# An attention and two feed-forward layers on one core: weights unpacked in place and ahead of the first product, with three smaller moves

## The chip, the core and the metric

The kernel runs on one core of one Trainium2 chip. The metric is the device time of one execution in microseconds (us), lower is better. TensorE (PE in the profile) multiplies; VectorE (DVE), ScalarE (ACT) and GpSimd (POOL) do elementwise work; SyncE (SP) mainly starts transfers. Each engine works through its own instructions in order, and waits for the others by semaphores.

## What is computed

```python
x  = attention(q, k, v, mem_k, mem_v)  # 4 batches x 8 heads x 768 positions x 64
#    chunks of 32 queries see 16 + 32 + 8 keys around them and 8 memory keys
x  = x.transpose(0, 2, 1, 3).reshape(3072, 512)
h  = x @ w_in                          # 512 x 2048
g  = maximum(h, 0) + log1p(exp(-abs(h)))
x1 = g @ w_out                         # 2048 x 512
y  = ((x1 @ w_a) * (x1 @ w_b)) @ w_o2  # 512 x 1536, twice, and 1536 x 512
```

The weights arrive as 64-bit floats, so the kernel unpacks them itself.

## The kernel before

The 3072 tokens are worked in 8 tiles of 384. Every product is made from a high and a low part of each operand, by three matrix products (high x high, high x low, low x high).

**Phase 1** (tiles t = 0 to 7, and in each f = 0 to 15): `ph` is one slice of x @ w_in, 12 matmuls (emit_h). The softplus follows on ACT (three activations, L462 to L464) and DVE (L466), ACT and POOL split it into `gh` and `gl` (L445, L446), and two slices later `px` adds it into the four accumulators of x1, 12 matmuls (emit_x1). After slice 15 the accumulators are copied out (`xo`, L484) and sent to DRAM. The next tile's `px` starts in the same four accumulators, so it waits for these copies. In phase 1 PE's order around a change of tiles is ph15, px13, ph0 of the next tile, px14, ph1, px15, ph2, px0. **Phase 2** does the same with w_a, w_b and w_o2, on x1 read back from DRAM.

**Weights.** A weight slice is 512 KB of raw words, in a buffer of the pool `w` (33 buffers, which hold raws, finished weights and much of the first attention). `convert_a` scales the upper words on ACT (L100) and joins upper and lower words on DVE (L102, L103) in a buffer `tmp`, of which there are two; `convert_b` rounds to the high part on ACT (L110) and gets the low part by a subtraction on POOL (L111). Tile 0 needs 32 weights: two are converted before the first `ph`, the others two per slice f. The 36 weights of phase 2 are converted in tile 7 and at the start of phase 2.

**Attention.** Tile 0's is done before the first `ph`, as 6 blocks of 64 queries. Their steps are woven by a table ROUND: round i does step s0 of block i, s1 of block i-1, and so on. s0 turns k and q on PE (`pt`), ACT and DVE copy the turned ones (L281, L285); s1 makes the scores (`scb`) and the exponentials; sn normalizes; s2 turns the result (`pat`); s3 multiplies by v (`pxb`) and places the block in the tile's x. SyncE starts the loads of k and q, ScalarE those of v.

For tiles 1 to 7 it is done as 21 units of 128 queries, three per tile, woven into the products of the tile ahead. A table of times in half slices sets the place of each step: turn (DVE transposes L354 to L357, two copies of the memory keys on GpSimd, L359), scores (`sc` on PE), soft, norm (POOL L334), flip (ten DVE transposes into `af`, L388), values (`pxa` on PE, L402) and place (ACT L409 writes x's high part, DVE L410 the low one). The last unit's place completes the x that the next tile's first `ph` reads.

For tile 0 the program fixes the order on all engines; from tile 1 on it fixes PE's, and a scheduler orders the others.

Of the kernel before, what the change touches and what calls it, by code (L numbers as in the profile page):

```python
# [9 lines left out]
F32 = mybir.dt.float32  # L10
F32R = mybir.dt.float32r
U32 = mybir.dt.uint32
AF = mybir.ActivationFunctionType
ALU = mybir.AluOpType
# [3 lines left out]
TT = 384  # L18
# [1 line left out]
LAG = 2  # L20
STEPS = ((-8, "turn"), (-5.3, "scores"), (-5, "soft"), (-3, "norm"), (-1, "flip"), (-0.9, "flip2"),
         (3, "values"), (3.1, "place"))
START = 2.4
SETS = 1
EARLY_STEPS = ((-6, "turn"), (-4.3, "scores"), (-4.2, "soft"), (-3, "norm"), (-0.7, "flip"), (1.3, "flip2"),
               (2, "values"), (2.9, "place"))
EARLY, EARLY_AT, EARLY_BY = 3, 13, 9
ROUND = ((0, "s0"), (1, "s1"), (2, "sn"), (3, "s3"), (2, "s2"))
CONVERT_AT = {21: "a0", 23: "b0", 25: "a1", 28: "b1"}
W_AT = {3: 1, 5: 2}  # L30
W_BY = (1, 2, 2, 2)
AHEAD = 10
LATE = 4
OUT_TAGS = "eegg"

# [2 lines left out]
def attn_moe_moe2(ctx: ExitStack, tc: tile.TileContext, q, k, v, mem_k, mem_v,  # L38
                  w_in, w_out, w_a, w_b, w_o2, out):
    nc = tc.nc  # L40
    B, H, S, D = q.shape
    M = mem_k.shape[2]
# [3 lines left out]
    P = 128  # L46
    CH, LC, RC = 32, 16, 8
    QB = 64
# [40 lines left out]
    def convert_a(dst, key):  # L89

        u, raw = dst[key]
        words = raw.rearrange("p (n two) -> p two n", two=2)
        low, high = words[:, 0], words[:, 1]
        top = high.bitcast(F32)
        val = mp.tile([P, 512], U32, tag="tmp", name=f"tmp{u}", bufs=2)

        nc.scalar.activation(top, top, AF.Prelu, scale=2.0 ** -112, alpha=-(2.0 ** 32))  # L100

        nc.vector.tensor_scalar(val, low, 29, None, ALU.logical_shift_right)  # L102
        nc.vector.scalar_tensor_tensor(val, high, 3, val, ALU.logical_shift_left, ALU.bitwise_or)  # L103
        dst[key] = u, val.bitcast(F32)

    def convert_b(dst, key, pool=None):

# [124 lines left out]
    def x_tile(t):  # L232
        if t not in xt:
            xt[t] = mp.tile([P, 2, KT, TT], F32R, tag="x", name=f"x{t}")
        return xt[t]
# [4 lines left out]
    class Block:  # L240
# [9 lines left out]
        def load(self):  # L250
            u = self.u
            qk = wp.tile([P, 2, H, D], F32, tag="w", name=f"qk{u}")
            if u % 2 == 0:
                first["v"] = wp.tile([P, 2, H, D], F32, tag="w", name=f"vv{u}")
            self.qn, self.kn, self.vn = qk[:QB, 0], qk[:KB, 1], first["v"][:KB, u % 2]
            s0 = QB * u - LC
            for t, src, mem in ((self.kn, k, mem_k), (None, q, None), (self.vn, v, mem_v)):
                if t is None:
                    nc.sync.dma_start(self.qn, q[0, :, QB * u:QB * u + QB, :].rearrange("h s d -> s h d"))
                    continue  # L260
                lo = max(s0, 0)
                go = nc.scalar.dma_start if src is v else nc.sync.dma_start
                go(t[lo - s0:CTX], src[0, :, lo:s0 + CTX, :].rearrange("h s d -> s h d"))
                if lo > s0:
                    go(t[0:lo - s0], src[0, :, 0:lo - s0, :].rearrange("h s d -> s h d"))
                go(t[CTX:KB], mem[0].rearrange("h m d -> m h d"))

        def s0(self):
            u = self.u
            work = wp.tile([P, 1024], F32, tag="w", name=f"work{u}")  # L270
            self.kt = work[:, :KT * KB].rearrange("p (i k) -> p i k", i=KT)
            self.sm = work[:, KT * KB:2 * KT * KB].rearrange("p (i k) -> p i k", i=KT)
            self.st = work[:, 2 * KT * KB:2 * KT * KB + 4 * KT].rearrange("p (n i) -> p n i", n=4)
            self.qt = qblk[:, u % 2]
            for m, (src, rows) in enumerate(((self.kn, KB), (self.qn, QB))):
                pt = self.psum(m, f"pt{m}_")[:, :KT * rows].rearrange("p (i t) -> p i t", i=KT)
                for i in range(KT):
                    nc.tensor.transpose(pt[:, i], src[:, 2 * i:2 * i + 2, :].rearrange("p h d -> p (h d)"),
                                        ident[:rows, :rows])
                if m == 0:  # L280
                    nc.scalar.copy(self.kt, pt)  # L281
                else:
                    for j in range(2):
                        r = slice(64 * j, 64 * j + 64)
                        nc.vector.tensor_copy(self.qt[r, :, r], pt[r])  # L285

        def s1(self):
            sc = self.psum(2, "scb")[:, :KT * KB].rearrange("p (i k) -> p i k", i=KT)
            for i in range(KT):
                nc.tensor.matmul(sc[:, i], lhsT=self.qt[:, i, :], rhs=self.kt[:, i, :], start=True, stop=True)  # L290
            softmax([sc], masks[3 if self.u == 0 else 1], self.sm, self.st)

        def sn(self):
            normalize(nc.vector, self.sm, self.st)

        def s2(self):
            u = self.u
            self.af = wp.tile([KB, KT, P], F32, tag="w", name=f"afb{u}")
            pa = self.psum(3, "pat")[:KB, :].rearrange("p (i t) -> p i t", i=KT)
            for i in range(KT):  # L300
                nc.tensor.transpose(pa[:, i], self.sm[:, i], ident)
            nc.scalar.copy(self.af, pa)

        def s3(self):
            u = self.u
            px = self.psum(4, "pxb")[:, :KT * QB].rearrange("p (i t) -> p i t", i=KT)
            x = x_tile(0)
            xh, xl = x[:, 0, :, u * QB:u * QB + QB], x[:, 1, :, u * QB:u * QB + QB]
            for i in range(KT):
                for j in range(2):  # L310
                    r = slice(64 * j, 64 * j + 64)
                    nc.tensor.matmul(px[r, i], lhsT=self.vn[:, 2 * i + j, :], rhs=self.af[:, i, r], start=True, stop=True)
            nc.scalar.copy(xh, px)
            nc.vector.tensor_tensor(xl, px, xh.bitcast(F32), ALU.subtract)

    first = {}

# [18 lines left out]
    class Unit:  # L336
# [10 lines left out]
        def turn(self):  # L347
            u, kn, qn = self.u, loaded.k, loaded.q
            n0 = 4 * (u % UPT)
            if self.n == 0 or u == UPT:  # L350
                nc.vector.transpose(out=mem_t, in_=mem_n)
            self.kt = a2.tile([P, KT, 2, KB], F32, tag="kt", name=f"kt{u}", bufs=1)
            self.qt = a2.tile([P, KT, QU], F32, tag="qt", name=f"qt{u}", bufs=1)
            nc.vector.transpose(out=self.kt[:, :, :, :64].rearrange("p i w (m s) -> p i w m s", m=2),  # L354
                                in_=kn[:, :, n0:n0 + 4].rearrange("p i (w m) d -> p i w m d", m=2))
            nc.vector.transpose(out=self.kt[:, :, :, 64:], in_=kn[:, :, n0 + 2:n0 + 5:2])
            nc.vector.transpose(out=self.qt, in_=qn[:, :, n0:n0 + 4].rearrange("p i n d -> p i (n d)"))  # L357
            for w in range(2):
                nc.gpsimd.tensor_copy(self.kt[:, :, w, CTX:], mem_t[:, :, :M])  # L359

        def scores(self):
            u = self.u
# [48 lines left out]

    blocks = [Block(u) for u in range(BPT)]
    units = [Unit(u) for u in range(B * NU)]

    att = []
    for i in range(BPT + 3):
        for d, step in ROUND:
            if 0 <= i - d < BPT:
                att.append(getattr(blocks[i - d], step))

    plan = []
    for i, unit in enumerate(units[UPT:]):
# [48 lines left out]
    def emit_x1(t, f):  # L471
# [9 lines left out]
        if f == NF1 - 1:  # L481
            for i in range(KT):
                o = mp.tile([P, TT], F32, tag=OUT_TAGS[i], name=f"xo{t}_{i}")
                (nc.vector.tensor_copy if i % 2 else nc.scalar.copy)(o, acc[t][i][:, :TT])  # L484
                nc.sync.dma_start(x1d[t, :, i, :], o)
            del acc[t]

# [52 lines left out]
    def order():  # L540
# [6 lines left out]
        def fetch_to(n):  # L547
            nonlocal n_w1
            while n_w1 < min(n, len(uses)):
                fetch1(n_w1)  # L550
                n_w1 += 1

        for i in range(BPT):
            blocks[i].load()
            fetch_to(W_AT.get(i, n_w1))
        for part in range(KT):
            loaded.fetch(1, part)
            fetch_to(n_w1 + W_BY[part])
        for i, step in enumerate(att):
            step()  # L560
            if i in CONVERT_AT:
                half, n = CONVERT_AT[i]
                (convert_a if half == "a" else convert_b)(*uses[int(n)])
        n_cv = 2

        def att_at(slot):
            while plan and plan[-1][0] <= slot:
# [6 lines left out]
        for t in range(NTILE):  # L574
# [9 lines left out]
            for f in range(NF1):  # L584
                ph = emit_h(t, f)
                if t == 0:
                    jobs = uses[n_cv:n_cv + 1 + (f + 2 < NF1)]
                    n_cv += len(jobs)
                    fetch_to(n_cv + AHEAD)
                    if len(jobs) == 2:  # L590
                        convert_a(*jobs[0])
                    emit_soft(t, f, ph, partial(convert_a, *jobs[-1]))
                    for job in jobs:
                        convert_b(*job)
                else:
                    emit_soft(t, f, ph)
                att_at(2 * (NF1 * t + f))
# [65 lines left out]
```

## Time and profile before

| what | value |
|---|---|
| median of three runs (lowest, highest) | 1346.58 us (1345.91, 1346.66) |
| the profiled execution: time, span | 1345.91 us, 1344.1 us |
| mean clock granted to PE, share of full speed | 0.979 |
| PE, ACT, DVE, POOL busy in the span | 93%, 39%, 34%, 30% |
| first `ph` starts | 59.16 us |
| tile 0, first `ph` to tile 1's first `ph` | 59.16 to 180.20 us |
| a tile from the second on (277.66 to 355.89) | 78.23 us |

The span is what the trace covers, and the execution takes 1.8 us more than it. Shares of the span say little by themselves, since the start, tile 0, the steady tiles and phase 2 have different limits. So the profile is read by stretches.

### The profile page before, as it was taken

What the parts mean: (1) busy time and instruction counts of PE and PEld (TensorE: products, weight loads), DVE (VectorE), ACT (ScalarE), POOL (GpSimd) and SP (SyncE); (2) the same over time, 40 slices, a digit from 0 to 9 for tenths busy, and PEclk for the clock granted to TensorE, in tenths of its full rate; (3) what the DMA queues carried; (4) which work ended last, traced back from release to release, by engine and by line L of the source; (5) the groups of instructions that cost most, each with busy time, mean ns of one, the idle gap of its engine ahead of it and who ended that gap; (6) DMA issues with size and microseconds to landing.
All of it is one profiled execution on the core that took longest, in us unless ns stands there. A gap on an engine that the chain in (4) does not pass through costs nothing.

```text
span 1344.1 us, 20011 instructions
## 1 busy us (share of the span) xinstructions
PE 1245.1 (93%) x7800; PEld 1176.7 (88%) x7800; DVE 460.6 (34%) x1188; ACT 530.8 (39%) x1296; POOL 401.6 (30%) x391
## 2 busy tenths in 40 slices
PE   3776859999999999999899999999999999999998
PEld 3666759989898998989888999999999999999997
DVE  2476863445345344434675601010101111010100
ACT  2575745555565555556577311111111111111111
POOL 1164732233223222223576612121212112121111
PEclk9987979999999999999999999999999999999999
DMA  8952232212131311210476101010100001000000
GB/s 155 254 184 74 48 89 51 38 46 49 47 61 35 55 29 48 47 46 12 136 238 215 46 1 48 0 47 1 40 9 24 24 1 47 1 24 0 25 0 24
DMA packets 170170, 77.99 MB, mean 58 GB/s; under 512 B 137691, under 2 KB 162395, under 8 KB 170075
## 3 DMA queue, kind: packets, MB, share of 16 engines
q1 hardware_dynamic: 164824, 75.46, 20.8%
q10 hardware_dynamic: 4739, 1.18, 0.6%
q8 instruction: 61, 1.00, 0.3%
q14 instruction: 34, 0.28, 0.1%
q0 software_dynamic: 512, 0.07, 0.0%
HBM read 64.09 MB, written 12.58 MB: 57 GB/s over the span
## 4 chain that ended last, share of the span: by engine, by line
PE 50%; DVE 2%; POOL 1%; issue 1%; ACT 1%; DMA 1%; ACTq 0%; DVEq 0%; POOLq 0%
PE pab L511 30%; PE py L531 15%; PE px L479 3%; PE ph L456 2%; DVE tmp L102 1%; POOL w L111 1%; DVE tmp L103 1%; DMA raw<-in_moe_w_out_dram 1%; ACT w L110 0%; DVE af L388 0%; ACT raw L100 0%; PE pxa L402 0%; DMA out_dram<-yo 0%; DVE g L466 0%; ACT e L463 0%
## 5 line engine op out<-in xcount | busy, mean ns | idle before, releaser
L511 PE MATMUL pab<-x,w 128*128 128x384 f32 x2304 | 417.2, 335 | 0.0
L511 PEld LDWEIGHTS pab<-x,w 128*128 128x128 f32 x2304 | 404.4, 188 | 8.2
L456 PE MATMUL ph<-x,w 128*128 128x384 f32 x1536 | 302.1, 345 | 12.4 <-POOL w L111 4.6
L456 PEld LDWEIGHTS ph<-x,w 128*128 128x128 f32 x1536 | 277.8, 195 | 18.7 <-DVE g L466 6.0
L520 DVE TENSOR_TENSOR c<-pab,a 128x384 f32<-128x384 f32 x96 | 53.5, 558 | 500.8 <-PE pab L511 499.8
L518 ACT COPY a<-pab 128x384 f32<-128x384 f32 x96 | 46.2, 481 | 251.7 <-PE pab L511 251.7
L466 DVE SCALAR_TENSOR_TENSOR g<-ph,e 128x384 f32<-128x384 f32 x128 | 71.2, 556 | 201.1 <-ACT e L464 199.3
L111 POOL TENSOR_TENSOR w<-tmp,w 128x512 fp32r<-128x512 f32 x68 | 88.6, 1318 | 76.2 <-ACT w L110 71.8
L462 ACT ACTIVATE e<-ph 128x384 f32<-128x384 f32 x128 | 62.3, 486 | 110.1 <-PE ph L456 109.9
L388 DVE STREAM_TRANSPOSE af<-sm 32x256 f32<-32x256 f32 x210 | 91.4, 435 | 21.1 <-POOL sm L334 18.2
L102 DVE TENSOR_SCALAR tmp<-raw 128x512 uint32<-128x512 uint32 x68 | 60.0, 882 | 34.2 <-POOL w L111 25.6
L464 ACT ACTIVATE e<-e 128x384 f32<-128x384 f32 x128 | 67.2, 525 | 3.7
L463 ACT ACTIVATE e<-e 128x384 f32<-128x384 f32 x128 | 67.2, 525 | 3.4
L103 DVE SCALAR_TENSOR_TENSOR tmp<-raw,tmp 128x512 uint32<-128x512 uint32 x68 | 62.4, 917 | 9.4 <-ACT raw L100 4.7
L327 ACT ACTIVATE sm<-sm,st 128x96 f32<-128x96 f32 x168 | 60.6, 362 | 7.0 <-DVE st L323 7.0
L110 ACT CAST w<-tmp 128x512 fp32r<-128x512 f32 x68 | 41.5, 618 | 28.1 <-DVE tmp L103 26.9
L100 ACT ACTIVATE raw<-raw 128x512 f32<-128x512 f32 x68 | 45.3, 667 | 17.6 <-DMA raw<-in_moe_w_b_dram 7.6
L323 DVE CUSTOM_DVE_ANT_0 sm<-sc,mask 128x96 f32<-128x96 f32 x168 | 32.3, 253 | 40.6 <-PE sc L370 40.6
L402 PEld LDWEIGHTS pxa<-af,vn 96*64 96x64 f32 x672 | 22.6, 143 | 25.3 <-DVE af L388 16.2
L402 PE MATMUL pxa<-af,vn 96*64 96x64 f32 x672 | 26.0, 231 | 19.6 <-DVE af L388 15.7
L479 PE MATMUL px<-g_0h,w 128*128 128x384 f32 x64 | 22.9, 398 | 22.4 <-DVE xo L484 21.2
L479 PEld LDWEIGHTS px<-g_0h,w 128*128 128x128 f32 x64 | 13.5, 213 | 25.8 <-DVE xo L484 24.2
(221 smaller groups left out, 1907.0 us busy)
## 6 DMA issues: line engine op xcount, KB each, us to landing
raw<-in_moe_w_out_dram SPq DMA_DIRECT2D x28, 512.0 KB
raw<-in_moe_w_in_dram SPq DMA_DIRECT2D x16, 512.0 KB
vn<-in_v_dram SPq DMA_DIRECT2D x35, 176.0 KB
raw<-in_moe_w_a_dram SPq DMA_DIRECT2D x12, 512.0 KB
raw<-in_moe_w_b_dram SPq DMA_DIRECT2D x12, 512.0 KB
x_scratch<-xo SPq DMA_DIRECT2D x32, 192.0 KB
xr<-x_scratch SPq DMA_DIRECT2D x8, 768.0 KB
out_dram<-yo SPq DMA_DIRECT2D x24, 256.0 KB
```

Of the source, the lines that this page charges most:

```text
L102: nc.vector.tensor_scalar(val, low, 29, None, ALU.logical_shift_right)
L103: nc.vector.scalar_tensor_tensor(val, high, 3, val, ALU.logical_shift_left, ALU.bitwise_or)
L111: nc.gpsimd.tensor_tensor(w[:, 1], val, w[:, 0].bitcast(F32), ALU.subtract)
L388: nc.vector.transpose(out=af[32 * kb:32 * kb + 32, x], in_=self.sm[32 * x:32 * x + 32, :, 32 * kb:32 * kb + 32])
L456: nc.tensor.matmul(ph, lhsT=a, rhs=c, start=n == 0, stop=n == 3 * KT - 1)
L462: nc.scalar.activation(e, ph, AF.Abs)
L463: nc.scalar.activation(e, e, AF.Exp, scale=-1.0)
L464: nc.scalar.activation(e, e, AF.Ln, bias=1.0)
L466: nc.vector.scalar_tensor_tensor(g, ph, 0.0, e, ALU.max, ALU.add)
L479: nc.tensor.matmul(acc[t][i][:, :TT], lhsT=a, rhs=c, start=f == 0 and m == 0, stop=f == NF1 - 1 and m == 2)
L511: nc.tensor.matmul(p, lhsT=a, rhs=c, start=n == 0, stop=n == 3 * KT - 1)
L531: nc.tensor.matmul(acc[t][i], lhsT=a, rhs=c, start=f == 0 and m == 0, stop=f == NF2 - 1 and m == 2)
```

## The change

1. `convert_a` works in the raw buffer. The two words of a number lie side by side, so what DVE writes, and what `convert_b` reads, now stands 8 bytes apart; the `tmp` buffers are gone, and a raw buffer is held until L111's successor is done with it.
2. ROUND gets a new order and one more round, and the conversions stand in it: a convert_a after the turn from round 1, a convert_b after the flip from round 2. Ten weights are converted ahead of the first `ph` (CV_AT), then 1.5 per slice f. The raw transfers go between the blocks' loads (EARLY_RAW).
3. SyncE, not ScalarE, starts the loads of v of the first blocks.
4. The four `xo` copies of a tile are all on VectorE (before: two on ScalarE).
5. The memory keys of the units are copied by ScalarE, not GpSimd.
6. Units have two sets of v (SETS), and from tile 1 on their steps come 0.8 half slices later (START); the three units in tile 0 keep their slots.

```diff
-START = 2.4
-SETS = 1
+START = 1.6
+SETS = 2
-ROUND = ((0, "s0"), (1, "s1"), (2, "sn"), (3, "s3"), (2, "s2"))
-CONVERT_AT = {21: "a0", 23: "b0", 25: "a1", 28: "b1"}
-W_AT = {3: 1, 5: 2}
-W_BY = (1, 2, 2, 2)
-AHEAD = 10
+ROUND = ((2, "normal"), (4, "place"), (0, "turn"), (2, "flip"), (1, "scores"), (3, "values"))
+EARLY_RAW = (0, 1, 2, 4, 6, 8)
+W_BY = (2, 2, 2, 2)
+AHEAD = 6
+CV_ROUND = 1
+CV_AT = (10, 1.5)
...
-        nc.vector.tensor_scalar(val, low, 29, None, ALU.logical_shift_right)
-        nc.vector.scalar_tensor_tensor(val, high, 3, val, ALU.logical_shift_left, ALU.bitwise_or)
-        dst[key] = u, val.bitcast(F32)
+        nc.vector.tensor_scalar(low, low, 29, None, ALU.logical_shift_right)
+        nc.vector.scalar_tensor_tensor(high, high, 3, low, ALU.logical_shift_left, ALU.bitwise_or)
+        dst[key] = u, top
...
-                go = nc.scalar.dma_start if src is v else nc.sync.dma_start
+                go = nc.sync.dma_start
...
-                nc.gpsimd.tensor_copy(self.kt[:, :, w, CTX:], mem_t[:, :, :M])
+                nc.scalar.copy(self.kt[:, :, w, CTX:], mem_t[:, :, :M])
...
-                (nc.vector.tensor_copy if i % 2 else nc.scalar.copy)(o, acc[t][i][:, :TT])
+                nc.vector.tensor_copy(o, acc[t][i][:, :TT])
...
+        for i in range(BPT + 4):
+            for d, step in ROUND:
+                if 0 <= i - d < BPT:
+                    getattr(blocks[i - d], step)()
+                if i >= CV_ROUND and step == "turn":
+                    convert_1(0)
+                if i > CV_ROUND and step == "flip":
+                    convert_1(1)
+        while n_cv[0] < CV_AT[0]:
+            convert_1(0)
+            convert_1(1)
...
-                    if len(jobs) == 2:
-                        convert_a(*jobs[0])
-                    emit_soft(t, f, ph, partial(convert_a, *jobs[-1]))
-                    for job in jobs:
-                        convert_b(*job)
+                    due = min(CV_AT[0] + int(CV_AT[1] * (f + 1)), len(uses))
+                    fetch_to(due + AHEAD)
+                    convert_1(0)
+                    emit_soft(t, f, ph, partial(convert_1, 1))
+                    while n_cv[0] < due:
+                        convert_1(0)
+                        convert_1(1)
```

Three places in the engines' orders bear on what follows. **PE at the change from tile 1 to tile 2**: `pxa` is the values step of the last unit that tile 2 needs, `ph_15` and `px_0` to `px_3` belong to tile 1, and `ph_0` is tile 2's first product. Before:

```order
L456 MATMUL ph_15_2409<-x_968,w_1455 128x384 x12
L402 MATMUL pxa_2432<-af,vn_83 64x64 x16
L479 MATMUL px_0_1775<-g_13h,w_1458 128x384
L479 MATMUL px_0_1775<-g_13l,w_1458 128x384
L479 MATMUL px_0_1775<-g_13h,w_1458 128x384
```

Now:

```order
L476 MATMUL px_3_1743<-g_13h,w_1439 128x384
L476 MATMUL px_3_1743<-g_13l,w_1439 128x384
L476 MATMUL px_3_1743<-g_13h,w_1439 128x384
L405 MATMUL pxa_2419<-af,vn_83 64x64 x16
L453 MATMUL ph_0_2438<-x_1860,w_316 128x384 x12
```

The unit's values stood ahead of the twelve matmuls of px13; they now stand behind them, with nothing between them and the product that reads the placed x. The same has moved at all six changes of tiles from 1 to 7; at the change from tile 0 to tile 1 it stood so already.

**DVE behind the change from tile 4 to tile 5** (`xo` are the accumulator copies, `af<-sm` the flips of the tile's first unit, `g` the softplus of the new tile). Before:

```order
L388 STREAM_TRANSPOSE af<-sm_5056 32x256 x8
L466 SCALAR_TENSOR_TENSOR g_1_5103<-ph_1_5086,e_1_5099 128x384
L388 STREAM_TRANSPOSE af<-sm_5056 32x256 x2
L484 COPY xo_1_5127<-px_1_4317 128x384
L484 COPY xo_3_5133<-px_3_4319 128x384
```

Now:

```order
L481 COPY xo_0_5100<-px_0_4283 128x384
L391 STREAM_TRANSPOSE af<-sm_5047 32x256 x3
L463 SCALAR_TENSOR_TENSOR g_1_5082<-ph_1_5065,e_1_5078 128x384
L481 COPY xo_2_5106<-px_2_4285 128x384
L391 STREAM_TRANSPOSE af<-sm_5047 32x256 x7
L481 COPY xo_1_5103<-px_1_4284 128x384
L481 COPY xo_3_5109<-px_3_4286 128x384
```

The copies xo_1 and xo_3 still stand behind all ten flips, and xo_0 and xo_2 now take their turn on the same engine ahead of them.

**DVE in tile 0 at slice 6** (`af<-sm` are the flips of unit 3, in two groups of five; `tmp` and `raw` are conversions). Before:

```order
L388 STREAM_TRANSPOSE af<-sm_749 32x256 x5
L102 TENSOR_SCALAR tmp_910<-raw_593 128x512
L103 SCALAR_TENSOR_TENSOR tmp_910<-raw_593,tmp_910 128x512
L466 SCALAR_TENSOR_TENSOR g_6_918<-ph_6_893,e_6_914 128x384
L102 TENSOR_SCALAR tmp_920<-raw_595 128x512
L103 SCALAR_TENSOR_TENSOR tmp_920<-raw_595,tmp_920 128x512
L388 STREAM_TRANSPOSE af<-sm_749 32x256 x5
```

Now:

```order
L391 STREAM_TRANSPOSE af<-sm_781 32x256 x5
L103 TENSOR_SCALAR raw_682<-raw_682 128x512
L104 SCALAR_TENSOR_TENSOR raw_682<-raw_682 128x512
L463 SCALAR_TENSOR_TENSOR g_6_935<-ph_6_913,e_6_931 128x384
L391 STREAM_TRANSPOSE af<-sm_781 32x256 x5
```

One conversion has gone from between the two groups of flips, as it has at every second slice; the flips themselves stand at the same slices.

## Rows read from the trace of the kernel before

**Rows 1.** Busy time by stretch; last three columns PE clock, DMA share, GB/s.

```profile
0.00:20.00 20.00, 3.05 (x16) 2.21 (x16) 4.12 (x40) 1.28 (x1) 4.79 (x16) 1.00 0.85 149
20.00:40.00 20.00, 15.56 (x96) 13.77 (x96) 7.69 (x44) 8.62 (x35) 0.00 (x0) 1.00 0.82 188
40.00:60.00 20.00, 14.69 (x112) 11.98 (x111) 10.72 (x42) 11.30 (x38) 2.55 (x2) 1.00 0.90 253
...
640.00:735.00 95.00, 84.89 (x493) 80.10 (x492) 64.33 (x79) 66.41 (x132) 58.31 (x45) 1.00 0.62 198
735.00:1344.00 609.00, 603.76 (x3182) 565.78 (x3180) 84.71 (x133) 113.24 (x228) 139.23 (x116) 1.00 0.06 22
```

**Rows 2.** Timeline, ScalarE then TensorE, start: time, length, instruction, [idle before].

```profile
20.95 0.28 ACTq L266 DMA_DIRECT2D vv<-in_mem_v_dram  x1
21.27 0.86 ACT L281 COPY work<-pt 128x384 f32<-128x384 f32 x2 [19.24 <-DMA qk<-in_mem_k_dram]
...
21.84 2.00 PE L290 MATMUL scb<-work,qblk 128*128 128x96 f32 x8 [10.23 <-issue]
...
41.92 1.46 PE L278 MATMUL pt<-ident,qk 96*128 96x96 f32 x8
...
59.16 1.15 PE L456 MATMUL ph<-x,w 128*128 128x384 f32 x2 [0.47 <-ACT x L313]
```

**Rows 3.** Waits of TensorE, 60 to 200 us: in total, times, longest.

```profile
PE pxa L402 <- DVE af L388: 15.7, 3, 6.8
PE sc L370 <- POOL kt L359: 11.0, 3, 5.6
PE ph L456 <- POOL w L111: 4.6, 3, 1.5
PE pxa L402 <- issue: 3.9, 2, 2.3
PE ph L456 <- ACT w L110: 1.7, 2, 1.2
```

**Rows 4.** Instruction groups by line, VectorE and GpSimd, 60 to 180 us.

```profile
L102 DVE TENSOR_SCALAR tmp<-raw 128x512 uint32<-128x512 uint32 x30 | 23.6, 786 | 9.6 <-POOL w L111 6.0 <-DMA raw<-in_moe_w_in_dram 2.1 <-DMA raw<-in_moe_w_a_dram 1.4
...
L111 POOL TENSOR_TENSOR w<-tmp,w 128x512 fp32r<-128x512 f32 x30 | 37.8, 1280 | 0.0
```

**Rows 5.** Timeline in tile 0, VectorE then GpSimd.

```profile
71.67 0.42 DVE L102 TENSOR_SCALAR tmp<-raw 128x512 uint32<-128x512 uint32 x1
...
75.02 1.50 DVE L102 TENSOR_SCALAR tmp<-raw 128x512 uint32<-128x512 uint32 x1 [2.13 <-POOL w L111]
...
73.71 2.52 POOL L111 TENSOR_TENSOR w<-tmp,w 128x512 fp32r<-128x512 f32 x2
```

**Rows 6.** Timeline at the changes of tiles, TensorE, ScalarE, VectorE.

```profile
180.20 0.69 PE L456 MATMUL ph<-x,w 128*128 128x384 f32 x1 [1.39 <-ACT x L409]
...
259.39 1.15 PE L402 MATMUL pxa<-af,vn 96*64 96x64 f32 x32
...
262.67 2.25 PE L456 MATMUL ph<-x,w 128*128 128x384 f32 x12
...
277.66 0.44 PE L479 MATMUL px<-g_0h,w 128*128 128x384 f32 x1 [2.88 <-DVE xo L484]
...
355.89 0.44 PE L479 MATMUL px<-g_0h,w 128*128 128x384 f32 x1 [2.89 <-DVE xo L484]
...
261.01 0.57 ACT L409 CAST x<-pxa 128x512 fp32r<-128x512 f32 x1
...
261.68 0.68 DVE L410 TENSOR_TENSOR x<-pxa,x 128x512 fp32r<-128x512 f32 x1
...
198.34 0.56 DVE L484 COPY xo<-px 128x384 f32<-128x384 f32 x1
```

**Rows 7.** Busy time behind the copies' wait; columns as in rows 1.

```profile
278.40:281.90 3.50, 3.50 (x13) 3.50 (x12) 0.40 (x1) 0.51 (x1) 1.00 (x1) 0.51 0.31 112
```

**Rows 8.** Waits of TensorE, 200 to 640 us.

```profile
PE px L479 <- DVE xo L484: 14.9, 6, 2.9
```

More of the change, by code (lines that the diff above doesn't have):

```diff
@@ L94, in convert_a @@
         top = high.bitcast(F32)
-        val = mp.tile([P, 512], U32, tag="tmp", name=f"tmp{u}", bufs=2)
         nc.scalar.activation(top, top, AF.Prelu, scale=2.0 ** -112, alpha=-(2.0 ** 32))
-        nc.vector.tensor_scalar(val, low, 29, None, ALU.logical_shift_right)
-        nc.vector.scalar_tensor_tensor(val, high, 3, val, ALU.logical_shift_left, ALU.bitwise_or)
-        dst[key] = u, val.bitcast(F32)
+        nc.vector.tensor_scalar(low, low, 29, None, ALU.logical_shift_right)
+        nc.vector.scalar_tensor_tensor(high, high, 3, low, ALU.logical_shift_left, ALU.bitwise_or)
+        dst[key] = u, top
     def convert_b(dst, key, pool=None):
@@ L266, in load, with turn @@
                 go(t[CTX:KB], mem[0].rearrange("h m d -> m h d"))
-        def s0(self):
+        def turn(self):
             u = self.u
@@ L285, in s0, with scores @@
                         nc.vector.tensor_copy(self.qt[r, :, r], pt[r])
-        def s1(self):
+        def scores(self):
             sc = self.psum(2, "scb")[:, :KT * KB].rearrange("p (i k) -> p i k", i=KT)
@@ L291, in s1, with normal, flip @@
             softmax([sc], masks[3 if self.u == 0 else 1], self.sm, self.st)
-        def sn(self):
+        def normal(self):
             normalize(nc.vector, self.sm, self.st)
-        def s2(self):
+        def flip(self):
             u = self.u
@@ L302, in s2, with values @@
             nc.scalar.copy(self.af, pa)
[L304 to L308, printed above, removed]
+        def values(self):
+            self.px = px = self.psum(4, "pxb")[:, :KT * QB].rearrange("p (i t) -> p i t", i=KT)
             for i in range(KT):
@@ L312, in s3, with place @@
                     nc.tensor.matmul(px[r, i], lhsT=self.vn[:, 2 * i + j, :], rhs=self.af[:, i, r], start=True, stop=True)
-            nc.scalar.copy(xh, px)
-            nc.vector.tensor_tensor(xl, px, xh.bitcast(F32), ALU.subtract)
+        def place(self):
+            u = self.u
+            x = x_tile(0)
+            xh, xl = x[:, 0, :, u * QB:u * QB + QB], x[:, 1, :, u * QB:u * QB + QB]
+            nc.scalar.copy(xh, self.px)
+            nc.vector.tensor_tensor(xl, self.px, xh.bitcast(F32), ALU.subtract)
     first = {}
@@ L413, in attn_moe_moe2 @@
     units = [Unit(u) for u in range(B * NU)]
[L415 to L419, printed above, removed]
     plan = []
@@ L554, in order @@
             blocks[i].load()
-            fetch_to(W_AT.get(i, n_w1))
+            fetch_to(EARLY_RAW[i])
         for part in range(KT):
@@ L558, in order, with convert_1 @@
             fetch_to(n_w1 + W_BY[part])
[L559 to L564, printed above, removed]
+        n_cv = [0, 0]
+        def convert_1(half):
+            if n_cv[half] < len(uses):
+                (convert_a, convert_b)[half](*uses[n_cv[half]])
+                n_cv[half] += 1
+        for i in range(BPT + 4):
[9 more added lines that the diff above has]
+            convert_1(1)
         def att_at(slot):
@@ L586, in order @@
                 if t == 0:
-                    jobs = uses[n_cv:n_cv + 1 + (f + 2 < NF1)]
-                    n_cv += len(jobs)
-                    fetch_to(n_cv + AHEAD)
-                    if len(jobs) == 2:
-                        convert_a(*jobs[0])
-                    emit_soft(t, f, ph, partial(convert_a, *jobs[-1]))
-                    for job in jobs:
-                        convert_b(*job)
+                    due = min(CV_AT[0] + int(CV_AT[1] * (f + 1)), len(uses))
[5 more added lines that the diff above has]
+                        convert_1(1)
+                    if due == len(uses):
+                        convert_1(1)
                 else:
```

## Prediction, made before the changed kernel ran

> **What bounds the kernel now.** I read the table of busy time by stretch first, because one share for the whole span hides stages with different limits. In the last 609 us TensorE is busy 603.76 us [rows 1]. That is phase 2 with its weights in place, nothing of the change touches it, and no gain can come from there. A steady tile takes 78.23 us from one wait for the accumulator copies to the next [rows 6], and from 200 to 640 us six of these waits, 14.9 us together, are all that TensorE waits for [rows 8]. Without the wait of 2.88 us, and without the 1.7 us that the stretch of some 3.4 us at half clock behind it costs [rows 6, 7], a tile with three units of attention is 73.7 us of TensorE work. That is the floor of tile 0 too, which has three units. But tile 0 takes 121.0 us, from 59.16 to 180.20 us [rows 2, 6]. So there are three places: the 59 us before the first product, the 47 us that tile 0 loses, and the changes of tiles.
>
> Before the first product, ScalarE is what stands still: its first copy of a turned block starts at 21.27 us, after 19.24 us without work, right behind the last v load that its own queue starts, at 20.95 us [rows 2]. TensorE meanwhile waits 10.23 us and goes on at 21.84 us. The page calls the releaser a transfer or "issue"; the rows' times say that it is ScalarE's queue.
>
> In tile 0, the list of waits names 15.7 and 3.9 us for the flips, 11.0 us for the memory keys that GpSimd copies, and 4.6 and 1.7 us for weights: 36.9 us [rows 3]. The other 10.4 us of the 47.3 are half clock behind such waits, and the place at its end.
>
> **The change, part by part.** The sum is made against the profiled 1345.91 us.
>
> *Before the first product.* The work of a block can start when its k and q are in. With the v loads on SyncE, ScalarE is free at once, and the limit becomes the transfers, which were busy 82 to 90% of this time already [rows 1]. Six blocks are 6 x 0.52 MB by their shapes, and six raws, 0.52 MB each, now stand ahead of the last block's k and q: 6.1 MB with that block's v left out. At 149 and 188 GB/s, the rates of the first two stretches [rows 1], the first 33 us bring 5.4 MB and 36 us bring all; at the 253 GB/s that larger transfers reach [rows 1] the raws go faster, so 32 to 36 us. From the last block's transposes to the first `ph` it took 17.2 us, from 41.92 to 59.16 us [rows 2]. The chain of steps stays the same, and the four further conversions woven into it each cost VectorE a little over 1 us, which I hide in its waits. So the first `ph` comes at 50 to 53 us, 51.5: **8 us gained**. Bounds: 3 (the conversions stand in the chain and nothing hides them) and 11.
>
> Here a rule speaks against a gain. The row above shows ScalarE standing still for 19.24 us behind its v loads, which are issues of 0.3 us each [rows 2]. The Trainium skill, "DMA: Bandwidth & Descriptors", section "Issuing engines are not separate DMA queues", says that all issuing engines end on the same 16 DMA engines, and that a second issuing engine saves only the sequencer's time, usually small. By that alone moving the loads would be worth some 4 us, 12 issues of 0.3 us, and the rest of the 8 nothing. The trace agrees about the 16 engines, but not about "small": an issue that has to wait holds up the copies queued behind it.
>
> *Tile 0, weights.* Ten weights are ready at the first `ph`; slice f needs 2f - 1 of them and at its start 10 + 1.5f are due. The waits for weights, 6.3 us, go. *Keys.* A copy on GpSimd stood behind two subtractions of 1.28 us per slice [rows 4], on ScalarE it stands behind activations of about half a microsecond. I leave 4 of 11.0 us: 7 gained (bounds 0 and 11). *Flips.* VectorE's order keeps the flips at their slices, and only one conversion in four leaves. The two-buffer wait goes: 6.0 us of VectorE's idle before L102 were for a GpSimd subtraction two conversions back [rows 4]. I take 5 of the 19.6 us (bounds 0 and 15). *Clock.* Of the 10.4 us I credit 3, since the longest waits stay. Together **21 us gained**, from 6 (weights alone) to 40 (near the floor).
>
> In-place working by itself: the operands lie 8 bytes apart now. VectorE already read them so, at 0.42 us [rows 5]. No row shows VectorE writing or GpSimd reading at that step, so the price is open: nothing, or up to a doubling of GpSimd's 1.28 us. I take nothing; the other end is a rival below.
>
> *Changes of tiles.* The last unit's values now stand directly before the product that reads its x, with nothing to cover the placing. In a steady tile the high part starts 0.47 us after the values end (259.39 + 1.15 to 261.01), takes 0.57, and the low part is done at 262.36 us, 1.8 us after the values [rows 6]. Today px13 lies over this and `ph` starts at 262.67 us without a wait. The change from tile 0 to 1 had the bare order already, and `ph` waited 1.39 us, and a little more for the low part [rows 6]. So 1.55 us each, six times: 9.3 us. The accumulator copies: two more copies of 0.56 us [rows 6] go ahead of xo_1 and xo_3 on VectorE, while part of the flips goes behind. At four of seven changes that is about 0.5 us more, at the first about 1 us, and at two about none, since xo_1 now comes ahead of the flips there: 3 us (bounds 0 and 8). Clock: the stretch at half clock behind the wait costs 1.7 us [rows 7]; with a second wait close before it I take 3 us in all (bounds 0 and 10). Together **15 us lost**, from 9 to 27. What the later steps would be for I can't find in the profile: no steady wait but the copies is there to remove.
>
> *Start of phase 2.* From 640 to 735 us TensorE is busy 84.89 of 95 us [rows 1], and its weights come through the same chain. The `tmp` wait goes, the raw buffers are held longer: **2 us gained**, from -4 to 6. Two v sets and the queue change of the later loads cost nothing: TensorE shows no wait for v.
>
> Sum: 8 + 21 + 2 - 15 = 16 us, so 1330 us for the profiled execution; the runs' median is 0.7 us above it, which I drop as smaller than any term.
>
> **The rivals.** A change of under 0.2%, 2.7 us, can't be told from none here.
>
> 1. *The conversions stay bound to GpSimd.* L102 takes 0.42 us alone and 1.50 us when it starts under a subtraction of GpSimd's pair from 73.71 to 76.23 us; its mean in tile 0 is 0.79 us [rows 4, 5]. In place or not, it meets the same subtractions. If that, and not the missing `tmp`, sets VectorE's pace, tile 0 gains the weights alone, 6 us: 8 + 6 + 2 - 15, 1345 us. Fewer conversions per slice speak against it. The Trainium skill's page "SBUF — State Buffer", section "SBUF: two separate sides", has this as an exclusive lock: a VectorE operation in a two-port mode and one of GpSimd block each other for the whole instruction. The trace agrees (0.42 against 1.50 us), and an edit in place wouldn't lift it.
> 2. *Half clock across each change.* If the new wait of 1.55 us and the next of some 3 us, 12 us later, bring TensorE to half clock for some 6 us more, each change costs 3 us more and all six 18: 1348 us. It decides from 2.7 us at each. For it: 3.4 us at half clock follow one wait of 2.88 us. Against it: the two waits have full work between them.
> 3. *GpSimd reads slowly at 8 bytes.* At 2.56 us for each subtraction, tile 0's 22 cost GpSimd 28 us more, of which I put 10 on the path, and the 36 of phase 2 cost 46 us more, of which tile 7 hides most and 10 stay: 1350 us, slower than before. The point at which it decides is some 80% more for each. Against it: ScalarE's L100 works at that step already and nothing in the profile shows it held up.
> 4. *Tile 0 reaches its floor*, some 40 us gained there: 1311 us. Against it: the flips keep their places, and the longest wait, 6.8 us, is one of theirs.
>
> **How the numbers follow.** My forecast, 16 us faster, gets 0.56, with its own range of 1320 to 1341; rival 1 gets 0.12, rival 2 0.13, rival 3 0.09 and rival 4 0.10. From these: faster 0.72 (nearly all of the forecast, rival 4, less than half of rival 1, a little of 2), within 0.2% 0.12, slower 0.16 (rival 3, and parts of 1 and 2). The range of 1312 to 1350 leaves out half of rival 4, half of rival 3 and some of rival 2, and takes in the bounds of tile 0 and the changes of tiles as long as not all fall the same way.
>
> **What would show it.** The first `ph` starts at 50 to 53 us, and ScalarE's first copy before 12 us. Tile 0 takes about 100 us, no wait of TensorE for L110 or the subtraction is left, and those for keys are under 2 us each. At six changes `ph` waits about 1.5 us for the placing, and the waits for the copies are about 3.4 us. GpSimd's subtraction takes 1.3 us; with 2 or more rival 3 is right. I am wrong if tile 0 stays above 112 us, or if the six tiles' period grows by over 5 us.

## The result, and the profile after

The changed kernel takes 1333.57 us (median of four runs, 1332.55 to 1334.83) against 1346.62 us, a ratio of 0.990 with a 95% interval of 0.989 to 0.992. The forecast was 1330 us. The profiled execution is the longest of the four, 1334.83 us with a span of 1333.0 us.

The timeline of the changed kernel, ScalarE's first copy and then TensorE: the last block's transposes, the first `ph`, and the first `ph` of tile 1 (line numbers are those of the changed kernel).

```profile
4.75 0.48 ACT L282 COPY work<-pt 128x384 f32<-128x384 f32 x1 [2.72 <-PE pt L279]
...
32.71 1.49 PE L279 MATMUL pt<-ident,qk 96*128 96x96 f32 x8 [0.64 <-DMA qk<-in_mem_k_dram]
...
49.61 0.69 PE L453 MATMUL ph<-x,w 128*128 128x384 f32 x1 [0.99 <-ACT x L316]
...
155.08 4.62 PE L453 MATMUL ph<-x,w 128*128 128x384 f32 x12 [0.69 <-ACT x L412]
```

Against [rows 2, 6], ScalarE copies 16.5 us earlier, the first `ph` comes 9.6 us earlier, and tile 1 starts 25.1 us earlier, so tile 0 took 105.5 us instead of 121.0. The first three rows of TensorE's waits from 48 to 200 us answer to [rows 3]. No wait for a weight is in the list any more; the units' scores and flips wait less, but they still wait.

```profile
PE pxa L405 <- DVE af L391: 11.8, 3, 5.2
PE sc L373 <- DVE qt L360: 7.2, 2, 3.9
PE pxa L405 <- issue: 3.6, 2, 1.9
```

Then half of the lead is given back. In the table of waits from 200 to 640 us there are three rows instead of the one of [rows 8]:

```profile
PE px L476 <- DVE xo L481: 17.0, 5, 3.5
PE ph L453 <- ACT x L412: 4.1, 6, 0.7
PE ph L453 <- DVE x L413: 1.7, 6, 0.3
```

and the timeline of TensorE at the change from tile 1 to tile 2 shows where they stand:

```profile
235.27 0.44 PE L453 MATMUL ph<-x,w 128*128 128x384 f32 x1 [0.68 <-ACT x L412]
236.00 2.20 PE L453 MATMUL ph<-x,w 128*128 128x384 f32 x11 [0.28 <-DVE x L413]
...
252.62 0.44 PE L476 MATMUL px<-g_0h,w 128*128 128x384 f32 x1 [3.51 <-DVE xo L481]
```

Tile 2's first `ph` comes at 235.27 us, before it was 262.67 [rows 6]; tile 7's at 638.05 against 652.30 us; the first product of phase 2 (`pab`) at 720.10 against 733.00 us. The last two, first in the changed kernel and then in the one before:

```profile
638.05 0.44 PE L453 MATMUL ph<-x,w 128*128 128x384 f32 x1 [0.69 <-ACT x L412]
720.10 4.34 PE L508 MATMUL pab<-x,w 128*128 128x384 f32 x24
...
652.30 1.03 PE L456 MATMUL ph<-x,w 128*128 128x384 f32 x5
733.00 1.20 PE L511 MATMUL pab<-x,w 128*128 128x384 f32 x6
```

So the lead of 27.4 us at tile 2 is 14.3 us at tile 7 and 12.9 us at phase 2. In the last 600 us, whose program hardly differs, the profiled run loses another 1.8 us; this changed kernel's profiled run is 1.3 us above its median and the one of before 0.7 us below its own, so I read nothing into it.

### The profile page after: what moved, and what is told of

The parts are those of the page before. It is cut to its first block, busy times and chain, and to the rows that moved or that the text cites. A ratio compares the mean times of both kernels' runs of the same rounds, so it can differ in the third digit from the quotient of the medians.

```text
span 1333.0 us, 20036 instructions
## 1 busy us (share of the span) xinstructions
PE 1247.3 (94%) x7800; PEld 1179.6 (88%) x7800; DVE 469.6 (35%) x1204; ACT 533.0 (40%) x1322; POOL 401.0 (30%) x349
## 4 chain that ended last, share of the span: by engine, by line
PE 78%; DVE 9%; ACT 5%; SPq 3%; issue 3%; DMA 1%; POOL 1%; DVEq 0%; ACTq 0%; POOLq 0%
PE pab L508 30%; PE ph L453 15%; PE py L528 15%; PE px L476 14%; DVE af L391 2%; DVE raw L104 2%; PE pxa L405 2%; DVE raw L103 1%; PE sc L373 1%; DVE g L463 1%; ACT sm L330 1%; SPq L267 1%; DVE xo L481 1%; ACT raw L101 1%; ACT e L460 1%
## 5 line engine op out<-in xcount | busy, mean ns | idle before, releaser
L453 PE MATMUL ph<-x,w 128*128 128x384 f32 x1536 | 305.0, 347 | 14.5 <-DVE g L463 5.6
L112 POOL TENSOR_TENSOR w<-raw,w 128x512 fp32r<-128x512 f32 x68 | 97.4, 1436 | 85.8 <-ACT w L111 85.6
L104 DVE SCALAR_TENSOR_TENSOR raw<-raw 128x512 uint32<-128x512 uint32 x68 | 69.1, 1019 | 16.6 <-ACT raw L101 12.9
L103 DVE TENSOR_SCALAR raw<-raw 128x512 uint32<-128x512 uint32 x68 | 56.3, 831 | 5.6 <-DMA raw<-in_moe_w_b_dram 1.9
L111 ACT CAST w<-raw 128x512 fp32r<-128x512 f32 x68 | 44.6, 655 | 22.1 <-POOL w L112 13.6
L337 POOL TENSOR_TENSOR sm<-sm,st 128x768 f32<-128x768 f32 x21 | 32.0, 1523 | 33.9 <-DVE st L335 28.0
L405 PE MATMUL pxa<-af,vn 96*64 96x64 f32 x672 | 25.9, 231 | 15.4 <-DVE af L391 11.8
```

The costliest lines, as they stand in the source:

```text
L103: nc.vector.tensor_scalar(low, low, 29, None, ALU.logical_shift_right)
L104: nc.vector.scalar_tensor_tensor(high, high, 3, low, ALU.logical_shift_left, ALU.bitwise_or)
L112: nc.gpsimd.tensor_tensor(w[:, 1], val, w[:, 0].bitcast(F32), ALU.subtract)
L405: nc.tensor.matmul(px[64 * j:64 * j + 64, i, QB * w:QB * w + QB], lhsT=vn[:, w, 2 * i + j], rhs=af[:, 2 * w:2 * w + 2, KT * j + i], start= ...
L453: nc.tensor.matmul(ph, lhsT=a, rhs=c, start=n == 0, stop=n == 3 * KT - 1)
```

## The experiments

Times are medians. Each run's ratio is to runs of the kernel before on the same chip. Kernels that were measured on different occasions are compared by these ratios.

**The units' later steps and the accumulator copies.** Three kernels are the changed one with one or both of these taken back, the fourth is the kernel before with the later steps alone.

```diff
-START = 1.6
+START = 2.4
...
-                nc.vector.tensor_copy(o, acc[t][i][:, :TT])
+                (nc.vector.tensor_copy if i % 2 else nc.scalar.copy)(o, acc[t][i][:, :TT])
```

> The changed kernel with the units' steps at their old times (START 2.4), all else as changed. Theory (the later steps only cost): the six waits for the placing, 0.97 us each in the changed kernel's trace, go, and the steady tiles' period falls from 80.6 us by 1 to 2 us; 1323 to 1329 us, ratio to before 0.983 to 0.987. Rival (the later steps pay for themselves, by flips that no longer stand ahead of the accumulator copies): no gain or a loss, 1332 to 1338 us.

> The changed kernel with the accumulator copies shared by ScalarE and VectorE again. Theory: the waits for the copies fall from 3.3 to 3.5 us back to about 2.9 us, six or seven times, and the half clock behind them does not lengthen: 3 to 6 us faster than changed, 1328 to 1331 us. Rival (the flips' place on VectorE alone sets these waits, not the number of copies): within 1.5 us of the changed kernel's 1333.6 us.

> Both taken back, START 2.4 and shared copies. Theory: the steady tiles come back to the 78.2 us of before, so the 25 us that the changed kernel is ahead at tile 1's first product stay until tile 7: 1319 to 1325 us, ratio 0.980 to 0.984. Rival (the tiles' lengthening has another cause, the raised load of ScalarE by the key copies or the two sets of v): the period stays above 79.5 us and the time above 1328 us.

> The kernel before with nothing but the later steps (START 1.6). Theory: six waits for the placing of about 1 us and a changed order of flips: 6 to 12 us slower than before, ratio 1.004 to 1.009. Rival (the later steps help where VectorE is in arrears, in tile 0's end): ratio 0.998 to 1.002.

Measured: START taken back 1327.26 us (ratio 0.985, interval 0.983 to 0.986); shared copies alone 1338.41 us (0.993, 0.991 to 0.994); both 1321.54 us (0.981, 0.979 to 0.982); the later steps on the kernel before 1356.13 us (1.006, 1.004 to 1.008). TensorE's waits from 200 to 640 us with START alone taken back:

```profile
PE px L476 <- DVE xo L481: 16.7, 5, 3.3
```

The six waits for the placing are gone. With both taken back only the copies' wait is left, back at its old length, and a tile takes 78.2 us again (174.56 to 252.79 us between two such waits):

```profile
PE px L476 <- DVE xo L481: 14.4, 5, 2.9
```

So the later steps cost 0.6%, 7 to 8 us, on either kernel, and with START 2.4 the VectorE copies cost another 0.4%. The first, third and fourth expectations came true. The second failed: with START 1.6, sharing the copies gave nothing. Of its five waits for the copies from 200 to 640 us the first two are 4.02 us and the others 2.88 us, and from tile 1's first `ph` to tile 7's it takes 482.9 us, as the changed kernel does (483.0). It loses its 0.3% at the start of phase 2, 86.0 us from tile 7's first `ph` against 82.1. In the traces the last copies stand behind a unit's flips on VectorE. When these start, and how many stand ahead of the copies, depends on both settings together.

**All copies where no flips stand.** START 2.4, and all four accumulator copies on ScalarE:

```diff
-                nc.vector.tensor_copy(o, acc[t][i][:, :TT])
+                nc.scalar.copy(o, acc[t][i][:, :TT])
```

> The changed kernel with START 2.4 and all four accumulator copies on ScalarE, where no flips stand. Theory (the waits for the copies are the flips ahead of them on VectorE, and the half clock behind follows from the wait): the six waits of 2.9 us and most of the 1.6 us of half clock behind each go, the period falls from 78.2 to 74 to 75 us: 1294 to 1304 us. Rival (the copies then stand behind the exponentials on ScalarE, and the next softplus behind the copies): the waits only change their name, 1315 to 1325 us.

Measured: 1298.17 us, ratio 0.963 (0.962 to 0.965), 23 us below the kernel with shared copies, as the theory said. The table of busy time from 200 to 600 us, to be held against the 14.9 us of waits of [rows 8] (after the length of the stretch, TensorE's busy time; third from the end its clock):

```profile
200.00:600.00 400.00, 400.00 (x3142) 388.08 (x3141) 182.32 (x599) 242.68 (x673) 114.47 (x108) 1.00 0.21 44
```

TensorE doesn't wait once in these 400 us, its clock doesn't fall, and ScalarE takes the copies at 242.68 busy of 400 us. A tile takes 73.6 us, by the timeline of two tiles' first `ph`:

```profile
231.81 2.25 PE L453 MATMUL ph<-x,w 128*128 128x384 f32 x12
...
305.39 2.25 PE L453 MATMUL ph<-x,w 128*128 128x384 f32 x12
```

With shared copies it took 78.2 us. So a wait of 2.9 us cost 4.6 us, with the stretch at half clock that followed it [rows 7], and 73.6 us is what the prediction called the floor, 73.7 us. At one of the changes the wait was as long, but no half clock followed: in the kernel before at 512.39 us, where the next tile's first `ph` came after 76.7 us instead of 78.2. Its busy time, to be held against [rows 7] (the clock is third from the end):

```profile
512.40:515.90 3.50, 3.50 (x20) 3.50 (x21) 0.96 (x2) 0.98 (x2) 1.11 (x2) 1.00 0.31 112
```

From tile 1's first `ph` to tile 7's the kernel with all copies on ScalarE takes 444.2 us, against 470.2 us with shared copies: 26.0 us less. From there to the first product of phase 2 it takes 83.4 against 80.2 us, so 3.2 us are given back; why isn't tested.

**In place alone.** The kernel before with part 1 of the change and nothing else (the three lines of `convert_a` in the diff above).

> The kernel before with nothing but the conversion in place. Theory: VectorE's wait for the second buffer goes, 6.0 us of idle time in tile 0 and 13.5 us at the start of phase 2, but little of it is on the path: 1341 to 1346 us. Rival (operands 8 bytes apart slow ScalarE's cast, GpSimd's subtraction and, held by them, VectorE; raw buffers come free later): 1348 to 1356 us.

Measured: 1349.23 us, ratio 1.001 (0.9997 to 1.002). The median lies in the range of the rival, but the runs of the kernel before that it is held against have 1347.56 us; by the ratio neither came true, there is no gain and no loss that the runs could tell. Groups of instructions by line, 58 to 180 us, VectorE's first shift and ScalarE's rounding, and then the rounding in the kernel before, 59 to 180 us:

```profile
L101 DVE TENSOR_SCALAR raw<-raw 128x512 uint32<-128x512 uint32 x29 | 21.2, 730 | 0.1
...
L109 ACT CAST w<-raw 128x512 fp32r<-128x512 f32 x30 | 19.9, 664 | 17.0 <-POOL w L110 11.2 <-DVE raw L102 4.7 <-POOL kt L358 0.7
...
L110 ACT CAST w<-tmp 128x512 fp32r<-128x512 f32 x30 | 18.5, 617 | 3.5 <-DVE tmp L103 2.8
```

VectorE's wait for GpSimd, 6.0 us in [rows 4], is gone (0.1 us idle), and ScalarE, which waited 3.5 us ahead of its roundings, now waits 17.0, of which 11.2 us are for GpSimd. By the program, a raw buffer now comes free only after GpSimd's subtraction, and the rounding needs a buffer of the same pool.

**Who starts the loads of v.** On the changed kernel the move is taken back, as shown; on the kernel before it is made alone, the same line the other way:

```diff
-                go = nc.sync.dma_start
+                go = nc.scalar.dma_start if src is v else nc.sync.dma_start
```

> The changed kernel with the blocks' v loads started by ScalarE again. Theory (ScalarE's queue is what stood still): its first copy starts at 15 us or later again, and the first product comes 5 to 9 us later than at 49.6 us: 1338 to 1343 us. Rival (the transfers set the pace, whoever starts them): first product within 2 us of 49.6 us, 1332 to 1336 us.

> The kernel before with nothing but the v loads started by SyncE. Theory (ScalarE's standing still is what the move takes away, 16 us in the changed kernel): ScalarE's first copy comes before 12 us, but the rounds still go at their pace of 6.07 us behind it: first product at 50 to 54 us against 59.2, tile 0 as before: 1338 to 1343 us. Rival (the move only pays with the new rounds and the raws between the loads, which make the issues wait longer): 1344 to 1348 us.

Measured: 1350.00 us (ratio 1.001, 1.000 to 1.002) with the loads back on ScalarE, so the whole gain is gone; 1337.81 us (0.993, 0.991 to 0.994) with the move alone on the kernel before. Both theories held in kind and were too small: taking the move back costs 14.5 us at the first product and not 5 to 9, and the move alone brings it to 48.31 us and not to 50 to 54. The timeline of the first of them, ScalarE's queue, its first copy, and TensorE:

```profile
25.37 0.41 ACTq L267 DMA_DIRECT2D vv<-in_mem_v_dram  x1
25.82 0.86 ACT L282 COPY work<-pt 128x384 f32<-128x384 f32 x2 [23.80 <-DMA qk<-in_k_dram]
...
26.40 2.00 PE L291 MATMUL scb<-work,qblk 128*128 128x96 f32 x8 [14.08 <-issue]
...
64.13 0.69 PE L453 MATMUL ph<-x,w 128*128 128x384 f32 x1 [1.00 <-ACT x L316]
```

and of the second:

```profile
4.94 0.48 ACT L281 COPY work<-pt 128x384 f32<-128x384 f32 x1 [2.92 <-PE pt L278]
...
48.31 2.11 PE L456 MATMUL ph<-x,w 128*128 128x384 f32 x5 [0.47 <-ACT x L313]
...
169.38 0.69 PE L456 MATMUL ph<-x,w 128*128 128x384 f32 x1 [1.37 <-ACT x L409]
```

The first of them shows the same picture as [rows 2]: the first copy follows the last issue of its own queue at once. The move brings the first product from 59.16 to 48.31 us by itself, with two weights converted and the old rounds, and tile 0 takes 121.1 us as before. In the changed order, with raw loads between the blocks' loads, ScalarE's last issue stands at 25.37 us instead of 20.95, and the first product comes at 64.13 us. What an issue waits for, no run shows.

**Ten weights ahead.** The changed kernel with two, and so with two per slice f instead of 1.5:

```diff
-CV_ROUND = 1
-CV_AT = (10, 1.5)
+CV_ROUND = 8
+CV_AT = (2, 2)
```

> The changed kernel with two weights instead of ten converted ahead of the first product, and two per slice. Theory (the conversions crowd tile 0): the first product comes 0 to 4 us earlier, at 46 to 50 us, but tile 0 takes 115 us or more against 105.5, with waits for weights and for the units' keys: 1338 to 1346 us. Rival (tile 0 gained by the key copies and the missing buffer wait, not by the ten): tile 0 under 108 us, 1328 to 1335 us.

Measured: 1357.30 us, ratio 1.007 (1.006 to 1.008), 23 us slower than the changed kernel by the ratios and further than I expected. The first `ph` comes at 50.45 us, 1.9 us of which it waits for its weight, so eight conversions more ahead of it cost nothing there. Tile 0 takes 126.9 us, to 177.34 us, and its waits, 48 to 178 us, are:

```profile
PE pxa L405 <- DVE af L391: 16.9, 3, 6.4
PE sc L373 <- DVE qt L360: 7.3, 3, 3.5
PE px L476 <- POOL w L112: 5.2, 6, 1.0
PE ph L453 <- ACT w L111: 4.2, 2, 2.2
PE ph L453 <- POOL w L112: 3.8, 7, 0.9
```

The weights' waits come back, and the flips' wait grows from 11.8 to 16.9 us; that it grows by the conversions in VectorE's queue is my reading. With 126.9 us tile 0 is 5.9 us longer than in the kernel before, so the other parts of the change together, without the ten ahead, gave it nothing.

**The units' memory keys.** The changed kernel with this copy on GpSimd.

```diff
-                nc.scalar.copy(self.kt[:, :, w, CTX:], mem_t[:, :, :M])
+                nc.gpsimd.tensor_copy(self.kt[:, :, w, CTX:], mem_t[:, :, :M])
```

> The changed kernel with the units' memory keys copied by GpSimd again. Theory (the prediction's 7 us): the scores of units 3 and 4 wait 9 to 11 us together for GpSimd against 7.2 us for VectorE now, 2 to 7 us slower than changed, 1335 to 1341 us. Rival (VectorE's transposes are late anyway, so the copy hides behind them): within 1.5 us of 1333.6 us.

Measured: 1333.88 us, ratio 0.989 (0.988 to 0.991), the same as the changed kernel. The waits of the scores, 49 to 157 us, have another name and 1.9 us more:

```profile
PE sc L373 <- POOL kt L362: 7.8, 2, 4.5
PE sc L373 <- DVE qt L360: 1.3, 1, 1.3
```

The rival held: VectorE's transposes are late whoever copies the keys.

**In place, in the new order.** The kernel of 1298 us with the two `tmp` buffers again (`convert_a` as before) and SETS = 1.

> The best kernel so far (START 2.4, copies on ScalarE, 1298 us) with the conversion through two tmp buffers again and one set of v, since both sets don't fit beside them. Theory (in place moved the wait from VectorE to ScalarE and gave nothing): within 3 us of 1298 us. Rival (with ten ahead and 1.5 per slice, in place does pay): 1303 to 1312 us.

Measured: 1310.56 us, ratio 0.972 (0.970 to 0.974), 12 us slower. The rival held. The group of the first shift, 50 to 158 us:

```profile
L104 DVE TENSOR_SCALAR tmp<-raw 128x512 uint32<-128x512 uint32 x25 | 19.3, 773 | 12.0 <-POOL w L113 11.9
```

VectorE waits 11.9 us for GpSimd again, and tile 0 ends at 166.68 instead of 155.58 us. The in-place kernel has in the same stretch:

```profile
L103 DVE TENSOR_SCALAR raw<-raw 128x512 uint32<-128x512 uint32 x25 | 19.9, 795 | 0.1
...
L111 ACT CAST w<-raw 128x512 fp32r<-128x512 f32 x25 | 16.3, 651 | 2.6 <-DVE raw L104 1.4 <-POOL w L112 0.6 <-DVE af L391 0.6
```

Here the wait has not moved to ScalarE: 0.6 us against the 11.2 above. By the profiled runs tile 0 takes 9.5 us more with `tmp` and one set (116.7 against 107.2 us), and tile 1 another 5.6 us (81.8 against 76.2). The kernels differ in the sets of v as well; TensorE's list of waits names no v load in either, but the two weren't tried apart, so how much of the 12 us is the missing `tmp` alone isn't shown.

**Earlier units in tile 0.** The kernel of 1298 us with EARLY_BY = 8 instead of 9, which brings tile 0's second unit half a slice and its third a whole slice forward.

> The best kernel so far with the second and third unit of tile 0 one slice earlier (EARLY_BY 8). Theory (the last unit's flips, 9.1 us of waits, come too late in tile 0, and its place is uncovered): tile 0 falls from 107 us by 3 to 8 us, 1290 to 1296 us. Rival (VectorE and the key loads are the limit there, so the waits only move): 1296 to 1302 us.

Measured: 1299.37 us, ratio 0.964 (0.963 to 0.965), no difference. The rival held in its outcome, by another way than the one named: the last unit's values end at 149.25 us, ahead of 24 more matmuls (twelve of `ph`, twelve of `px`), but ScalarE stands from 149.8 to 154.84 us in front of a conversion for phase 2 whose raw transfer hasn't landed, and the place is queued behind it. Its timeline, and TensorE's wait at tile 1's first `ph`:

```profile
154.84 0.68 ACT L101 ACTIVATE raw<-raw 128x512 f32<-128x512 f32 x1 [5.07 <-DMA raw<-in_moe_w_a_dram]
...
158.05 0.58 ACT L412 CAST x<-pxa 128x512 fp32r<-128x512 f32 x1
...
158.68 0.45 PE L453 MATMUL ph<-x,w 128*128 128x384 f32 x1 [3.58 <-ACT x L412]
```

## Why the prediction was right, point by point

The sum was 16 us and the medians give 13.1. The places and the mechanisms were mostly right; the sizes were not, and that the sum came so close is in part luck: tile 0 gave 5.4 us less than forecast, and the changes of tiles cost 4.1 us less.

- *Before the first product*, 8 us forecast, 9.6 measured. The last block's transposes at 32.71 us lie in the 32 to 36 us worked out from the transfers, and the chain behind them took 16.9 us against 17.2. The v loads' move does all of this: alone it gave 10.9 us at the first product, so the new rounds, with eight conversions more ahead of it, gave nothing further there; they weren't tried alone. ScalarE's 13 issues of v take 4.6 us together in the kernel before, but the copies behind them waited until the last had gone. The Trainium skill, "DMA: Bandwidth & Descriptors", section "Issuing engines are not separate DMA queues", calls the sequencer's time that is saved by a second issuing engine usually small. The two runs decide otherwise for this kernel, 10.9 and 14.5 us.
- *Tile 0*, 21 us forecast, 15.6 measured, and 105.5 us where the prediction said about 100. The waits for weights went, 6.3 us, as said, and the flips' waits fell by 4.2 us (19.6 to 15.4) where 5 were credited. The step on the keys failed in its reason: 7 us were credited to ScalarE's copying, and the run with GpSimd's copies is no slower. The scores' wait fell by 3.8 us, from 11.0 to 7.2, and what is left is named as a wait for VectorE's transposes, up to 3.9 us where under 2 was forecast. TensorE also has a new wait of 1.3 us right behind the first `ph`, for the low part of the last block's x. What carries tile 0 is the ten weights ahead (126.9 us without, 105.5 with).
- *Rival 1, the conversions stay bound to GpSimd*, was right about the parts. In place alone gains nothing. The second shift, which reads two operands, takes 0.69 us where no work of GpSimd lies beside it and up to 1.77 us where some does; its mean was 0.80 us in the kernel before and is 1.01 now. Groups of the changed kernel, 49 to 155 us:

```profile
L104 DVE SCALAR_TENSOR_TENSOR raw<-raw 128x512 uint32<-128x512 uint32 x26 | 26.4, 1014 | 11.2 <-ACT raw L101 9.7
L103 DVE TENSOR_SCALAR raw<-raw 128x512 uint32<-128x512 uint32 x26 | 20.7, 797 | 0.4 <-DMA raw<-in_moe_w_a_dram 0.4
...
L112 POOL TENSOR_TENSOR w<-raw,w 128x512 fp32r<-128x512 f32 x27 | 39.3, 1460 | 37.4 <-ACT w L111 37.3
```

  The first shift's mean is what it was, 0.80 against 0.79 us [rows 4]. This agrees with the exclusive lock that the Trainium skill, "SBUF — State Buffer", section "SBUF: two separate sides", describes. Rival 1 fell as a forecast because the order, and not the buffers, took conversions out of tile 0; with that order, on the best kernel, going back to `tmp` and to one set of v costs about 12 us.
- *Rival 3, slow reading at 8 bytes*, is out. GpSimd's shortest subtraction took 1.28 us against 1.26, and ScalarE's rounding 0.66 against 0.62 us; the longer mean, 1.46 against 1.28 us, comes with VectorE's shifts beside it: of the 26 that start from 49 to 155 us, five have none beside them and take 1.30 us on average, the 21 others 1.51.
- *Changes of tiles*, 15 us forecast. From the start of tile 1 to that of tile 7 the lead fell by 10.9 us; from tile 2 on, where the first change with its old order is left out, by 13.1 us, 2.6 us a tile. The mechanisms are those named, the sizes not. The place waits 0.97 us and not 1.55. The 1.39 us of [rows 6] was no good measure: at that change, in the kernel before, a conversion, late because its raw words were, stood ahead of the place on ScalarE, and the kernel before with START 1.6 waits 0.69 us there. The timeline of ScalarE in the kernel before:

```profile
179.00 0.68 ACT L100 ACTIVATE raw<-raw 128x512 f32<-128x512 f32 x1 [2.98 <-DMA raw<-in_moe_w_a_dram]
179.56 0.58 ACT L409 CAST x<-pxa 128x512 fp32r<-128x512 f32 x1
```

  The copies wait 0.5 to 0.6 us more, as said. Most of the remaining 1.1 us a tile is half clock. By the granted clock, TensorE stands at half clock for 3.4 us behind four of the five changes from 277 to 590 us before, and behind one not at all; in the changed kernel it does so for 3.4 us behind three of the five from 252 to 575 us and for 6.9 us behind the other two, 10.3 us more in all, which at half clock is 5.1 us of work or 1.0 us a tile. Two stretches of the changed kernel at the copies' waits that end at 412.88 and 492.91 us show the two kinds (the clock is third from the end):

```profile
412.00:418.00 6.00, 5.12 (x20) 5.12 (x21) 1.81 (x4) 0.51 (x1) 1.00 (x1) 0.72 0.19 68
492.00:498.00 6.00, 5.09 (x16) 5.09 (x17) 1.84 (x4) 0.51 (x1) 1.01 (x1) 0.52 0.19 67
```

  The prediction had taken 3 us in all for this, 0.5 us a change, and it was twice that; rival 2, 3 us more at each change, did not come. The prediction's remark that nothing in the profile asks for the later steps was right: they only cost.
- *Start of phase 2*, 2 us gained by forecast, 1.3 us lost, from tile 7's first `ph` to the first product of phase 2. No run looks for the cause.

## What to carry to other kernels

An engine that starts transfers among its own work stands still whenever an issue does; look at the last issue on its queue and the first instruction behind it before blaming the transfers. Taking a wait away by working in place only helps if the buffer that is now held longer isn't needed by the next engine; in one order of this kernel 6.0 us of waits on VectorE went and 11.2 us on ScalarE came; in another, going back (with one set of v besides) cost 12 us. When copies wait behind a burst of other work in an engine's queue, give all of them to the engine without the burst: sharing them left the wait as it was here (2.9 us), all of them on ScalarE took it away.

## What the runs showed of the hardware that was not expected

The first `ph` of seven kernels with the same program up to there, or nearly the same, came at 48.35 to 51.11 us. The last block's transposes scatter by 2.0 us of these 2.8, 32.09 to 34.09 us, so most of it is there before the chain behind them begins; what makes it isn't shown. Differences of this size at the first product say nothing about an edit. And a wait of 2.9 us of TensorE cost 4.6 us in a tile where the half clock followed it, 3.1 us at the one change where it didn't.
